# Token mixing's first matrix moved past tokens as weights, its output transposed through DRAM

## The chip, the cores and the metric

The kernel runs on one core of a Trainium2 chip. A core has five engines that run side by side, each in the order of its own instructions: TensorE (PE) for matmuls, VectorE (DVE), ScalarE (ACT) and GpSimd (POOL) for work on elements, and SyncE (SP), which here only issues DMA transfers. TensorE reads both operands from SBUF and writes to PSUM, eight banks of 2 KB per partition. The metric is the device time of one execution in microseconds, lower is better.

## What is computed

The input x is 2048 tokens by 448 channels. Branch A is attention with 16 query heads of 28 and one shared key and value head. Branch B is a mixer: token mixing, then an MLP. A gate from x mixes both. The part that matters here is token mixing:

```python
h = _gelu(_layernorm(x, axis=-1) @ w1)          # 448 x 448
c = D // 4
g0 = jnp.pad(h[:, :, 0*c:1*c], ((0, 0), (1, 0), (0, 0)))[:, :S, :]   # shift +1
g1 = jnp.pad(h[:, :, 1*c:2*c], ((0, 0), (0, 1), (0, 0)))[:, 1:, :]   # shift -1
...
hs = jnp.concatenate([g0, g1, g2, g3], axis=-1) @ w2
x1 = x + hs
```

Each quarter of the 112 channels of h is shifted by 1 or 2 tokens before w2.

## The kernel before, in words

Tokens are worked on in four blocks of 512 (`NB`), channels in four chunks of 128 (the last has 64 and carries the low part of its own in the other 64 partitions). Every product that needs precision is made from a high and a low part of each operand (`ah`/`al`, `w1h`/`w1l`, `hh`/`hl`), so that a block of `w1` takes 4 x 11 matmuls.

Stage 1 (lines 262 to 665) makes, on PE in the order of the program text:

- `stage_q(u)`, u = 0 to 15 (block times group of heads): queries, keys, values and the gate, with 11 matmuls each. `q_out` copies the result on ACT and sends it to DRAM (`qd`) from ACT's queue, the last one from SP's.
- `stage_w1(b)`, lines 442 to 468: h of block b, channels on partitions. For each of four groups of 112 channels, 11 matmuls with the weights of w1 as the stationary operand and 512 tokens moving; DVE multiplies by the inverse deviation of each token, which must stand along the free axis (`rsb`); ACT applies the gelu twice, once rounded (`hh`) and once not (`hf`); POOL subtracts (`hl`). The mean is taken out beforehand by centring w1 (`centre_w1`). `ln1_send` and `ln1_read` (lines 379 to 390) bring the deviations to that form: a PE transpose, an ACT copy, a write to DRAM and a broadcast read.
- `spare_h(b)` fills the 16 unused partitions of `hh` and `hl` with rows of the low part by four small DMAs, `spare_w2` does so for w2.
- `stage_w2(b)`, lines 470 to 482: for each of four tiles of 128 tokens, 11 matmuls of 448 columns with `hh`/`hl`, read at a shifted offset, as the stationary operand. The result is added to x1 by DVE. Its PSUM tiles come from `hs_tile`, which has two banks, so the third tile needs the add of the first.
- `stage_kv(b)`: eight DMAs that bring the keys of block b from `qd` to `kl` and two that bring values and gate to `vT`, on SP. `stage_v` transposes vT on PE.

`mm1` gives the PSUM tiles of `stage_q` and `stage_w1`, four in turn. The order of stage 1 is q0 to q11, w1(0), w1(1), w2(0), w1(2), w2(1), q12 to q15, w1(3), w2(2) with `stage_v` behind its first tile, w2(3). All engines keep the order of the program text (`manual_schedule`). Functions called `between` put work of other engines between the tiles of a stage.

The MLP's first input makes a similar trip already: `layernorm_norm` transposes blocks of 32 x 32 on DVE, `xt_write` writes them to DRAM in four DMAs (`xd`), `xt_read` reads them back with channels on partitions (`xr`), and `ln_split` copies them in a rearranged order.

Tiles with one tag share `bufs` buffers in turn; a new tile waits until the oldest is no longer used. Behind stage 1 come the MLP (lines 667 to 767) and the attention (from line 770), 785 us in which nothing of the text changes.

Of the kernel before, what the change touches and what calls it, by code (L numbers as in the profile page):

```python
# [9 lines left out]
F32 = mybir.dt.float32  # L10
F32R = mybir.dt.float32r
BF16 = mybir.dt.bfloat16
AF = mybir.ActivationFunctionType
ALU = mybir.AluOpType
# [3 lines left out]
P = 128  # L18
# [19 lines left out]
def f32(ap):  # L38
    return ap.bitcast(F32)
# [3 lines left out]
def gated_mix_kernel(  # L43
# [45 lines left out]
    def misc_tile(name):  # L89
        return psA.tile([P, 512], F32, tag="misc", bufs=1, name=name)  # L90
# [18 lines left out]
    def split_w_high(raw, wh, wl):  # L109
        nc.scalar.copy(wh[:, 0:3, :], raw[:, 0:3, :])  # L110
        nc.gpsimd.memset(f32(wh)[64:128, 3, :], 0.0)
        nc.scalar.copy(wh[0:64, 3, :], raw[0:64, 3, :])
        nc.scalar.copy(wl[64:128, 3, :], raw[64:128, 3, :])

    def split_w_low(raw, wh, wl):
        for c in range(3):
            nc.vector.tensor_tensor(wl[:, c, :], raw[:, c, :], f32(wh)[:, c, :], ALU.subtract)
        nc.vector.tensor_tensor(wl[0:64, 3, :], raw[0:64, 3, :], f32(wh)[0:64, 3, :], ALU.subtract)
# [14 lines left out]
    def proj(ps, wh, wl, ah, al):  # L133
        for c in range(3):
            nc.tensor.matmul(ps, wh[:, c, :], ah[:, c, :], start=(c == 0), stop=False)  # L135
            nc.tensor.matmul(ps, wh[:, c, :], al[:, c, :], start=False, stop=False)  # L136
            nc.tensor.matmul(ps, wl[:, c, :], ah[:, c, :], start=False, stop=False)  # L137
        nc.tensor.matmul(ps, wh[:, 3, :], ah[:, 3, :], start=False, stop=False)  # L138
        nc.tensor.matmul(ps, wl[:, 3, :], ah[:, 3, :], start=False, stop=True)  # L139
# [8 lines left out]
        nc.gpsimd.tensor_tensor(rs, rs, powt, ALU.pow)  # L148

    def stats_tiles(pool, b):  # L150
        return (pool.tile([P, 4, 2], F32, tag="mv", bufs=2, name=f"mv_{pool.name}_{b}"),
                pool.tile([P, 4], F32, tag="rs", bufs=2, name=f"rs_{pool.name}_{b}"))

    def layernorm_stats(pool, b):
        mv, rs = stats_tiles(pool, b)
# [106 lines left out]
    with tc.tile_pool(name="s1b", bufs=1) as s1b, \  # L262
# [5 lines left out]
        def mm1(name):  # L268
            k = turn[0] % 4
            turn[0] += 1  # L270
            return mm_tile(name) if k < 2 else ps1.tile([P, 512], F32, tag="tp", bufs=2, name=name)
# [6 lines left out]
        def load_x(b):  # L278
            if b == 1:
                xraw[b] = f32(s1b.tile([P, 4, 512], F32R, tag="w2x", bufs=1, name="xkv_1"))  # L280
            else:
                xraw[b] = s1.tile([P, 4, 512], F32, tag="raw", bufs=2, name=f"xkv_{b}")
            nc.sync.dma_start(xraw[b], xT[:, :, 512 * b:512 * b + 512])
# [12 lines left out]
            if c == 0:  # L296
                nc.sync.dma_start(wqraw[:, c, 256:512], wq[:, c, 256:512])
        nc.scalar.activation(first, powt, AF.Gelu_apprx_tanh)
        w1h = s1.tile([P, 4, 512], F32R, name="w1h")
        w1l = s1.tile([P, 4, 512], F32R, name="w1l")  # L300
        w2h = s1b.tile([P, 4, D], F32R, name="w2h")
        w2l = s1b.tile([P, 4, D], F32R, name="w2l")
        hh, hl, acts = {}, {}, {}
# [61 lines left out]
            nc.vector.tensor_copy(vext[:, :, 1:1 + DH].rearrange("p (b t) d -> p t b d", t=4), vp[:, :, :, 0:DH])  # L365
            nc.vector.tensor_copy(gz.rearrange("p (b t) -> p t b", t=4), vp[:, :, :, DH])

        rb_of = {}

        rs1_of = {}  # L370

        def ln1_tile(b, t):
# [2 lines left out]
            stats_tile(s1, b, t, rs1_of[b][0])  # L375
            if t == 3:
                stats_end(*rs1_of[b])

        def ln1_send(b):
            ps = misc_tile(f"rsT_{b}")[0:4, 0:P]  # L380
            nc.tensor.transpose(ps, rs1_of.pop(b)[1], ident)
            rT = s1.tile([4, P], F32, tag="rT", bufs=2, name=f"rT_{b}")
            nc.scalar.copy(rT, ps)
            rb_of[b] = dram.tile([4, P], F32, tag="rsd", bufs=2, name=f"rsd_{b}")
            nc.sync.dma_start(rb_of[b], rT)

        def ln1_read(b):
            rd = rb_of[b]
            rb_of[b] = s1.tile([P, 512], F32, tag="rsb", bufs=2, name=f"rsb_{b}")
            nc.sync.dma_start(rb_of[b][0:C], rd.rearrange("(o t) p -> o (t p)", o=1).broadcast_to([C, 512]))  # L390

        ones = s1.tile([P, P], F32, name="ones")
        nc.gpsimd.memset(ones, 1.0)
# [16 lines left out]
        def high_w2(m):  # L410
            nc.scalar.copy(w2h[0:C, m, :], w2raw[0:C, m, :])
            if m:
                nc.gpsimd.tensor_copy(w2x[0:C, m, :], f32(w2h)[0:C, m, :])

        def spare_w2():
            high = f32(w2h)
            nc.sync.dma_start(high[C:P, 0:2, :], high[0:32, 0, :])
            nc.sync.dma_start(high[C:P, 2:4, :], high[32:64, 0, :])
            nc.sync.dma_start(f32(w2x)[C:P, 1:3, :], high[64:96, 0, :])
            nc.sync.dma_start(f32(w2x)[C:P, 3, :], high[96:112, 0, :])  # L420
# [11 lines left out]
        def spare_h(b):  # L432
            low = f32(hl[b])
            nc.sync.dma_start(shifted(hh[b], 0, 2), low[0:32, 0, 1:513])
            nc.sync.dma_start(shifted(hh[b], 2, 2), low[32:64, 0, 1:513])
            nc.sync.dma_start(shifted(hl[b], 1, 2), low[64:96, 0, 1:513])
            nc.sync.dma_start(shifted(hl[b], 3, 1), low[96:112, 0, 1:513])

        def low_w2(m):
            nc.vector.tensor_tensor(w2l[0:C, m, :], w2raw[0:C, m, :], f32(w2h)[0:C, m, :], ALU.subtract)  # L440

        def stage_w1(b, between=None):
            hh[b] = s1b.tile([P, 4, 516], F32R, tag="hh", bufs=2, name=f"hh_{b}")
            hl[b] = s1b.tile([P, 4, 516], F32R, tag="hl", bufs=2, name=f"hl_{b}")
            for tt in (hh, hl):
                if b == 0:
                    nc.gpsimd.memset(f32(tt[b])[0:C, :, 0:2], 0.0)
                else:
                    nc.gpsimd.tensor_copy(tt[b][0:C, :, 0:2], f32(tt[b - 1])[0:C, :, 512:514])
            for m in range(4):  # L450
                ps = mm1(f"h_{b}_{m}")
                w = slice(m * P, m * P + C)
                proj(ps[0:C, :], w1h[:, :, w], w1l[:, :, w], *xact[b])
                if between:
                    between(m)
                hf = s1.tile([P, 512], F32, tag="hf", bufs=3, name=f"hf_{b}_{m}")
                nc.vector.tensor_mul(hf[0:C, :], ps[0:C, :], rb_of[b][0:C, :])
                nc.scalar.activation(hh[b][0:C, m, 2:514], hf[0:C, :], AF.Gelu_apprx_tanh)
                nc.scalar.activation(hf[0:C, :], hf[0:C, :], AF.Gelu_apprx_tanh)
                nc.gpsimd.tensor_tensor(hl[b][0:C, m, 2:514], hf[0:C, :], f32(hh[b])[0:C, m, 2:514],  # L460
                                        ALU.subtract)
            if b in (0, 2):
                spare_h(b)
            for tt in (hh, hl):
                if b:
                    nc.gpsimd.tensor_copy(tt[b - 1][0:C, :, 514:516], f32(tt[b])[0:C, :, 2:4])
                if b == NB - 1:
                    nc.gpsimd.memset(f32(tt[b])[0:C, :, 514:516], 0.0)

        def stage_w2(b, between=None):  # L470
            for t in range(4):
# [42 lines left out]
        centre_w1()  # L514
        stage_q(7)
        stage_q(8)
        w1_views = [f32(w1raw).rearrange("p c (m j) -> p c m j", j=C)]
        w1_views += [w.rearrange("p c (m j) -> p c m j", j=P)[:, :, :, 0:C] for w in (w1h, w1l)]
        split_w_high(*w1_views)
        split_w_low(*w1_views)  # L520
        for t in range(4):
            ln1_tile(1, t)
        stage_q(9)
        ln1_send(0)
        ln1_read(0)
        load_x(3)
        stage_q(10)
        load_x1(3)
        stage_q(11)
        high_w2(0)  # L530
        high_w2(1)

        def first_between(m):
            low_w2(m)
            if m < 2:
                high_w2(m + 2)
            if m == 2:
                ln1_send(1)
                ln1_read(1)
                spare_w2()  # L540

        stage_w1(0, first_between)

        def second(m):
            if m < 2:
                high_x(3, 2 * m, 2 * m + 2)
            if m in (1, 2):
                split_x(3, 2 * m - 2, 2 * m, False)
            else:
                ln1_tile(2, 2 * m // 3)  # L550
                ln1_tile(2, 2 * m // 3 + 1)

        stage_w1(1, second)
        stage_kv(0)
        stage_kv(1)
        spare_h(1)

        def third(t):
            if t == 2:
                ln1_send(2)  # L560
                ln1_read(2)
            if t < 3:
                ln1_tile(3, t)

        stage_w2(0, third)
        stage_kv(2)
        ln1_tile(3, 3)
        mv0, rs0 = stats_tiles(s1, "m")
        stage_w1(2, lambda t: stats_tile(s1, 0, t, mv0))
        stats_end(mv0, rs0)  # L570
        ln1_send(3)
        ln1_read(3)
        xt4 = s1.tile([P, 2048], F32, tag="raw", bufs=2, name="xt4")[:, 0:4 * D].rearrange(
            "p (f t j) -> p f t j", f=NE, t=4)

# [3 lines left out]

        stage_w2(1, norm_first)  # L580
        xt_write(0, xt4)
        for u in range(12, 16):
            stage_q(u)
        stage_w1(3)
        stage_kv(3)
        s1_stack.close()

# [54 lines left out]

        xraw2[0] = big("xr_0").rearrange("p (c n) -> p c n", c=4)
        xt_read(0, xraw2[0])
        spare_h(NB - 1)
        load_w34(0, s2a)

        def third(t):
# [496 lines left out]
```

## Time and profile before

| | |
|---|---|
| median of 3 runs | 911.44 us (911.14 to 912.0) |
| span of the profiled execution | 909.7 us |
| PE, share of the span busy | 99% |
| ACT | 70% |
| DVE | 57% |
| POOL | 9% |

The span runs from the first to the last instruction of the profiled execution; the page gives no other time of that execution, and the runs' times include what lies around the span.

A row of a timeline has the start in us, the duration in us, the engine, the line of the kernel, the operation, output<-input, shape and count, and in brackets the idle time before it and what ended it. A row of a group has the count, then the busy time and the mean duration in ns, then the idle time of the engine before its instructions and the releasers. A row of waits has the total in us, the number of times and the longest. `SPq` and `ACTq` are the queues from which SP and ACT issue DMAs. Matmuls overlap, so that their durations are longer than the distance of their starts.

### The profile page before, as it was taken

The numbers are of one execution on the slowest core, as the hardware profiler recorded it, in microseconds if no ns is written. First come the engines' busy times: TensorE is split into PE (matmuls) and PEld (weight loads), VectorE is DVE, ScalarE is ACT, GpSimd is POOL, SyncE is SP. The second block draws the span as 40 slices with busy tenths as digits, with TensorE's granted clock in tenths as the row PEclk, the third lists the DMA queues.
The fourth block names the chain that finished last, engine by engine and source line by source line (L and its number), as shares of the span: only waits on it lengthen the run. The fifth ranks groups of instructions, "written<-read, shape, count | busy, mean of one in ns | idle before, by whom it ended". The sixth has DMA issues, their size and how long they took to land.

```text
span 909.7 us, 24149 instructions
## 1 busy us (share of the span) xinstructions
PE 903.1 (99%) x10360; PEld 626.8 (69%) x10360; DVE 515.8 (57%) x960; ACT 632.6 (70%) x1003; POOL 79.1 (9%) x116
## 2 busy tenths in 40 slices
PE   9999999999999999999999999999999999999998
PEld 6788888888888888875555555555555555555554
DVE  3665273631441531136766777676767667767665
ACT  5542444332132231269999999999999999999995
POOL 3243320200000520020000000000000000000000
PEclk9999999999999999999999999999999999999999
DMA  8832653120110120010000001000011000010001
GB/s 294 289 103 61 147 167 129 37 70 1 39 49 2 22 65 1 1 52 24 14 25 14 24 15 56 23 25 17 25 33 36 24 14 25 15 55 14 15 14 44
DMA packets 40726, 47.31 MB, mean 52 GB/s; under 512 B 10152, under 2 KB 28904, under 8 KB 40616
## 3 DMA queue, kind: packets, MB, share of 16 engines
q1 hardware_dynamic: 37448, 40.43, 15.2%
q10 hardware_dynamic: 3168, 5.31, 1.6%
q8 instruction: 82, 1.34, 0.6%
q14 instruction: 28, 0.23, 0.1%
HBM read 32.56 MB, written 11.67 MB: 49 GB/s over the span
## 4 chain that ended last, share of the span: by engine, by line
PE 97%; ACT 2%; DMA 1%; DVE 0%; issue 0%; SPq 0%
PE bank L893 26%; PE bank L204 20%; PE bank L844 6%; PE acc L701 5%; PE acc L699 5%; PE acc L700 5%; PE g L135 4%; PE g L137 4%; PE g L136 4%; PE pair L204 2%; ACT p L257 2%; PE hs L475 1%; PE hs L476 1%; PE g L138 1%; PE g L139 1%; PE h L136 1%
## 5 line engine op out<-in xcount | busy, mean ns | idle before, releaser
L257 ACT ACTIVATE p<-bank 128x512 f32<-128x512 f32 x514 | 265.9, 605 | 4.4 <-POOL pick L866 1.5
L893 PE MATMUL bank<-p,vext 128*32 128x256 f32 x4064 | 247.7, 382 | 1.0 <-ACT p L257 1.0
L893 PEld LDWEIGHTS bank<-p,vext 128*32 128x32 f32 x4064 | 117.9, 110 | 115.9 <-ACT p L257 53.0
L954 DVE COPY p<-pair 128x1024 f32<-128x1024 f32 x125 | 153.0, 1224 | 57.9 <-PE pair L204 40.9
L689 ACT ACTIVATE gh<-g 128x512 fp32r<-128x512 f32 x55 | 32.9, 598 | 181.7 <-PE g L139 181.7
L818 DVE TENSOR_TENSOR o<-o,bank 128x256 f32<-128x256 f32 x222 | 93.5, 421 | 80.4 <-PE bank L893 72.3
L257 ACT ACTIVATE p<-p 128x1024 f32<-128x1024 f32 x126 | 138.0, 1096 | 0.0
L257 ACT ACTIVATE p<-pair 128x1024 f32<-128x1024 f32 x129 | 136.8, 1060 | 0.0
L691 DVE TENSOR_TENSOR gl<-gf,gh 128x512 fp32r<-128x512 f32 x55 | 38.6, 702 | 164.9 <-ACT gf L690 164.9
L204 PE MATMUL bank<-qh,kh 32*128 32x512 f32 x514 | 114.8, 443 | 0.0
L204 PE MATMUL pair<-qh,kh 32*128 32x512 f32 x510 | 114.0, 443 | 0.0
L204 PE MATMUL bank<-qh,kl 32*128 32x512 f32 x514 | 101.8, 389 | 0.0
L204 PE MATMUL bank<-ql,kh 32*128 32x512 f32 x514 | 101.6, 390 | 0.0
L204 PE MATMUL pair<-qh,kl 32*128 32x512 f32 x510 | 101.3, 389 | 0.0
L204 PE MATMUL pair<-ql,kh 32*128 32x512 f32 x510 | 100.9, 389 | 0.0
L204 PEld LDWEIGHTS bank<-qh,kh 32*128 32x128 f32 x514 | 48.0, 182 | 61.3 <-issue 38.7
L701 PE MATMUL acc<-w4h,gl 128*128 128x448 f32 x220 | 80.7, 367 | 0.0
L699 PE MATMUL acc<-w4h,gh 128*128 128x448 f32 x220 | 80.2, 364 | 0.0
L700 PE MATMUL acc<-w4l,gh 128*128 128x448 f32 x220 | 79.8, 363 | 0.0
L844 PE MATMUL bank<-wof,on 128*32 128x224 f32 (+1 forms) x984 | 69.6, 357 | 0.0
L135 PE MATMUL g<-ah,w3h 128*128 128x512 f32 x168 | 65.4, 389 | 0.0
L136 PE MATMUL g<-al,w3h 128*128 128x512 f32 x168 | 65.4, 389 | 0.0
(206 smaller groups left out, 1394.1 us busy)
## 6 DMA issues: line engine op xcount, KB each, us to landing
qd<-qf ACTq DMA_DIRECT2D x15, 256.0 KB
rb<-rd SPq DMA_DIRECT2D x15, 256.0 KB
x<-in_x_dram SPq DMA_DIRECT2D x4, 896.0 KB
xd<-xt SPq DMA_DIRECT2D x16, 224.0 KB
w34raw<-in_w_dram SPq DMA_DIRECT2D x7, 512.0 KB
qr<-qd SPq DMA_DIRECT2D x64, 56.0 KB
w34raw<-in_w_dram SPq DMA_DIRECT2D x7, 448.0 KB
out_dram<-ot SPq DMA_DIRECT2D x14, 224.0 KB
```

What stands on the lines that cost most here:

```text
L135: nc.tensor.matmul(ps, wh[:, c, :], ah[:, c, :], start=(c == 0), stop=False)
L136: nc.tensor.matmul(ps, wh[:, c, :], al[:, c, :], start=False, stop=False)
L204: nc.tensor.matmul(ps[j], k[h, keys], q[h, :], start=(r == 0), stop=(r == 2), tile_position=(32 * j, 0))
L257: nc.scalar.activation(p[:, heads], p[:, heads] if source is None else source, AF.Exp, scale=SCALE)
L691: nc.vector.tensor_sub(gl, gf, f32(gh))
L699: nc.tensor.matmul(ps, gh[:, tok], w4h[i][:, k, :], start=(f == 0), stop=False)
L700: nc.tensor.matmul(ps, gh[:, tok], w4l[i][:, k, :], start=False, stop=False)
L701: nc.tensor.matmul(ps, gl[:, tok], w4h[i][:, k, :], start=False, stop=(f == stop))
L818: nc.vector.tensor_add(o, o, pv)
L844: nc.tensor.matmul(ps[32 * i:32 * i + 32, :], a[:, c:c + 32], w, start=start, stop=stop, tile_position=(0, 32 * i))
L893: nc.tensor.matmul(pv[32 * j:32 * j + 32, :], vext[:, kt, :], p_of[k][:, j, qs], start=(k == ks[0]), stop=(k == ks[-1]), tile_position=(0, ...
L954: nc.vector.tensor_copy(pa[:, both], pairs[0])
```

## The change

The operands of w1's product change sides: a tile of 128 tokens of x is the stationary operand, and the 448 columns of w1 move, so that h comes out with tokens on partitions. The inverse deviation is then one number per partition and goes into the gelu's `scale`. `ln1_send`, `ln1_read` and their tiles are gone. DVE transposes h in blocks of 32 x 32 into `ht`; four DMAs write it to DRAM (`hd`), one reads it back with channels on partitions (`h_read`, into `hraw`, one buffer); `h_part` copies it into `hh` on ACT and subtracts into `hl` on DVE (even groups) or POOL (odd ones). `spare_h` is now issued behind the first group.

The order becomes q0 to q11, w1(0), w1(1), w1(2), q12, w2(0), w1(3), w2(1), q13 to q15, w2(2), w2(3); `stage_kv` of blocks 0 to 2 moves ahead of w1(0). x of block 3 is loaded into a buffer of `hraw`'s, `w1h` and `w1l` get 448 columns instead of 512, and `mv` and `rs` a third buffer.

```diff
         def load_x(b):
...
+            elif b == 3:
+                xraw[b] = s1.tile([P, 4, 512], F32, tag="hraw", bufs=1, name="xkv_3")
...
-        def stage_w1(b, between=None):
+        hd_of, hraw_of = {}, {}
+
+        def stage_w1(b, between=None, after=None):
+            ht = s1.tile([P, 2048], F32, tag="raw", bufs=2, name=f"ht_{b}")[:, 0:4 * D].rearrange(
+                "p (f t j) -> p f t j", f=NE, t=4)
+            ah, al = xact[b]
+            for t in range(4):
+                tok = slice(t * P, (t + 1) * P)
+                ps = mm1(f"h_{b}_{t}")[:, 0:D]
+                for c in range(3):
+                    nc.tensor.matmul(ps, ah[:, c, tok], w1h[:, c, :], start=(c == 0), stop=False)
+                    nc.tensor.matmul(ps, al[:, c, tok], w1h[:, c, :], start=False, stop=False)
+                    nc.tensor.matmul(ps, ah[:, c, tok], w1l[:, c, :], start=False, stop=False)
+                nc.tensor.matmul(ps, ah[:, 3, tok], w1h[:, 3, :], start=False, stop=False)
+                nc.tensor.matmul(ps, ah[:, 3, tok], w1l[:, 3, :], start=False, stop=True)
+                if between:
+                    between(t)
+                hf = s1.tile([P, 512], F32, tag="hf", bufs=3, name=f"hf_{b}_{t}")[:, 0:D]
+                nc.scalar.activation(hf, ps, AF.Gelu_apprx_tanh, scale=rs1_of[b][1][:, t:t + 1])
+                nc.vector.transpose(ht[:, :, t, :], hf.rearrange("p (f j) -> p f j", j=32))
+                if after:
+                    after(t)
+            hd_of[b] = dram.tile([NE, 32, 4, 128], F32, tag="hd", bufs=2, name=f"hd_{b}")
+            for p in range(4):
+                nc.sync.dma_start(hd_of[b][:, :, p].rearrange("f i u -> i f u"),
+                                  ht[32 * p:32 * p + 32].rearrange("i f t j -> i f (t j)"))
+
+        def h_read(b):
+            hraw_of[b] = s1.tile([P, 4, 512], F32, tag="hraw", bufs=1, name=f"hraw_{b}")
+            nc.sync.dma_start(hraw_of[b][0:C], hd_of.pop(b).rearrange("f i p u -> (f i) (p u)").rearrange(
+                "(m r) u -> r m u", m=4))
...
-            for m in range(4):
-                ps = mm1(f"h_{b}_{m}")
...
+        def h_part(b, m):
+            raw = hraw_of[b][0:C, m, :].rearrange("n (p t j) -> n p t j", p=4, t=4)
+            hi, lo = [tt[b][0:C, m, 2:514].rearrange("n (t p j) -> n p t j", p=4, t=4) for tt in (hh, hl)]
+            nc.scalar.copy(hi, raw)
+            (nc.gpsimd if m % 2 else nc.vector).tensor_tensor(lo, raw, f32(hi), ALU.subtract)
+
+        def h_parts(b, m0, m1):
+            if m0 == 0:
+                h_begin(b)
+            for m in range(m0, m1):
+                h_part(b, m)
+                if m == 0:
+                    spare_h(b)
...
         high_w2(0)
         high_w2(1)
+        for b in range(3):
+            stage_kv(b)
...
+        stage_w1(0, in_first)
+        h_read(0)
...
+        stage_w1(1, in_second)
+        stage_w1(2, None, lambda t: t in (1, 2) and h_parts(0, 2 * t - 2, 2 * t))
+        h_read(1)
+        stage_q(12)
+
+        def in_w2_first(t):
+            if t < 2:
+                h_parts(1, 2 * t, 2 * t + 2)
             if t < 3:
                 ln1_tile(3, t)
 
-        stage_w2(0, third)
-        stage_kv(2)
+        stage_w2(0, in_w2_first)
         ln1_tile(3, 3)
+        h_read(2)
         mv0, rs0 = stats_tiles(s1, "m")
-        stage_w1(2, lambda t: stats_tile(s1, 0, t, mv0))
+        stage_w1(3, lambda t: stats_tile(s1, 0, t, mv0), lambda t: t < 2 and h_parts(2, 2 * t, 2 * t + 2))
         stats_end(mv0, rs0)
-        ln1_send(3)
-        ln1_read(3)
+        h_read(3)
...
         stage_w2(1, norm_first)
         xt_write(0, xt4)
-        for u in range(12, 16):
-            stage_q(u)
-        stage_w1(3)
+        stage_q(13)
+        h_parts(3, 0, 2)
+        stage_q(14)
+        h_parts(3, 2, 4)
+        stage_q(15)
         stage_kv(3)
         s1_stack.close()
```

More of the change, by code (lines that the diff above doesn't have):

```diff
@@ L150, in stats_tiles @@
     def stats_tiles(pool, b):
-        return (pool.tile([P, 4, 2], F32, tag="mv", bufs=2, name=f"mv_{pool.name}_{b}"),
-                pool.tile([P, 4], F32, tag="rs", bufs=2, name=f"rs_{pool.name}_{b}"))
+        return (pool.tile([P, 4, 2], F32, tag="mv", bufs=3 if pool.name == "s1" else 2, name=f"mv_{pool.name}_{b}"),
+                pool.tile([P, 4], F32, tag="rs", bufs=3 if pool.name == "s1" else 2, name=f"rs_{pool.name}_{b}"))
     def layernorm_stats(pool, b):
@@ L298, in gated_mix_kernel @@
         nc.scalar.activation(first, powt, AF.Gelu_apprx_tanh)
-        w1h = s1.tile([P, 4, 512], F32R, name="w1h")
-        w1l = s1.tile([P, 4, 512], F32R, name="w1l")
+        s1.tile([P, 16], F32, name="gap_w1")
+        w1h = s1.tile([P, 4, D], F32R, name="w1h")
+        w1l = s1.tile([P, 4, D], F32R, name="w1l")
+        s1.tile([P, 48], F32, name="gap_x")
         w2h = s1b.tile([P, 4, D], F32R, name="w2h")
@@ L366, in stage_v @@
             nc.vector.tensor_copy(gz.rearrange("p (b t) -> p t b", t=4), vp[:, :, :, DH])
-        rb_of = {}
         rs1_of = {}
@@ L377, in ln1_tile @@
                 stats_end(*rs1_of[b])
[L379 to L390, printed above, removed]
         ones = s1.tile([P, P], F32, name="ones")
@@ L440, in low_w2, with h_begin @@
             nc.vector.tensor_tensor(w2l[0:C, m, :], w2raw[0:C, m, :], f32(w2h)[0:C, m, :], ALU.subtract)
-        def stage_w1(b, between=None):
+        hd_of, hraw_of = {}, {}
[27 more added lines that the diff above has]
+                "(m r) u -> r m u", m=4))
+        def h_begin(b):
             hh[b] = s1b.tile([P, 4, 516], F32R, tag="hh", bufs=2, name=f"hh_{b}")
@@ L449, in stage_w1 @@
                     nc.gpsimd.tensor_copy(tt[b][0:C, :, 0:2], f32(tt[b - 1])[0:C, :, 512:514])
-            for m in range(4):
-                ps = mm1(f"h_{b}_{m}")
[L452 to L468, printed above, removed]
+        def h_part(b, m):
[10 more added lines that the diff above has]
+                    spare_h(b)
+            if m1 == 4:
+                for tt in (hh, hl):
+                    if b:
+                        nc.gpsimd.tensor_copy(tt[b - 1][0:C, :, 514:516], f32(tt[b])[0:C, :, 2:4])
+                    if b == NB - 1:
+                        nc.gpsimd.memset(f32(tt[b])[0:C, :, 514:516], 0.0)
         def stage_w2(b, between=None):
@@ L516, in gated_mix_kernel @@
         stage_q(8)
[L517 to L520, printed above, removed]
+        split_w_high(w1raw, w1h, w1l)
+        split_w_low(w1raw, w1h, w1l)
         for t in range(4):
@@ L523, in gated_mix_kernel @@
         stage_q(9)
-        ln1_send(0)
-        ln1_read(0)
         load_x(3)
@@ L531, in gated_mix_kernel, with in_first, in_second @@
         high_w2(1)
[L533 to L539, printed above, removed]
-                spare_w2()
[L542 to L561, printed above, removed]
+        for b in range(3):
+            stage_kv(b)
+        def in_first(t):
+            low_w2(t)
+            if t < 2:
+                high_w2(t + 2)
+            if t == 2:
+                spare_w2()
+            if t == 3:
+                ln1_tile(2, 0)
+                ln1_tile(2, 1)
+        stage_w1(0, in_first)
+        h_read(0)
+        def in_second(t):
+            if t < 2:
+                high_x(3, 2 * t, 2 * t + 2)
+            if t in (1, 2):
+                split_x(3, 2 * t - 2, 2 * t, False)
+            if t in (0, 3):
+                ln1_tile(2, 2 + t // 3)
+        stage_w1(1, in_second)
[3 more added lines that the diff above has]
+        def in_w2_first(t):
+            if t < 2:
+                h_parts(1, 2 * t, 2 * t + 2)
             if t < 3:
                 ln1_tile(3, t)
-        stage_w2(0, third)
-        stage_kv(2)
+        stage_w2(0, in_w2_first)
         ln1_tile(3, 3)
+        h_read(2)
         mv0, rs0 = stats_tiles(s1, "m")
-        stage_w1(2, lambda t: stats_tile(s1, 0, t, mv0))
+        stage_w1(3, lambda t: stats_tile(s1, 0, t, mv0), lambda t: t < 2 and h_parts(2, 2 * t, 2 * t + 2))
         stats_end(mv0, rs0)
-        ln1_send(3)
-        ln1_read(3)
+        h_read(3)
         xt4 = s1.tile([P, 2048], F32, tag="raw", bufs=2, name="xt4")[:, 0:4 * D].rearrange(
@@ L644, in gated_mix_kernel @@
         xt_read(0, xraw2[0])
-        spare_h(NB - 1)
         load_w34(0, s2a)
```

## The prediction

> **What bounds the kernel now.** I read the page first, then stage 1 (0 to 125 us), the only stretch that the change touches, engine by engine in time.
>
> ```profile
> span 909.7 us, 24149 instructions
> PE   9999999999999999999999999999999999999998
> PE 97%; ACT 2%; DMA 1%; DVE 0%; issue 0%; SPq 0%
> ```
>
> PE is busy in every slice and makes 97% of the chain that ended last. The span is the profiled execution's own; the runs' median, 911.44, is 1.7 above it, and I add changes of the span to the median. As nothing ends later than PE, an edit is worth what it changes in PE's own time plus every wait that it puts in front of PE. PE takes its work in program order, so a wait of one matmul is a wait of all behind it.
>
> PE's timeline (start, duration, line) gives the pace as the distance of starts, since the durations overlap:
>
> ```profile
> 44.22 0.39 PE L139 MATMUL h<-ahk,w1l 128*112 128x512 f32 x1
> ...
> 44.47 0.48 PE L135 MATMUL h<-ahk,w1h 128*112 128x512 f32 x1
> 44.78 0.40 PE L136 MATMUL h<-alk,w1h 128*112 128x512 f32 x1
> ...
> 57.15 0.37 PE L475 MATMUL hs<-w2h,hh 128*128 128x448 f32 x1
> ...
> 63.90 0.27 PE L381 MATMUL rsT<-ident,rs_s 128*4 128x128 f32 x1
> ...
> 95.77 0.39 PE L135 MATMUL h<-ahk,w1h 128*112 128x512 f32 x1
> ...
> 105.86 0.36 PE L475 MATMUL hs<-w2h,hh 128*128 128x448 f32 x1
> ...
> 108.10 0.60 PE L363 MATMUL vp<-ident,vT 128*128 128x128 f32 x4
> ```
>
> From 95.77 to 105.86 run the 44 matmuls of one w1 block, 512 columns each: 10.09 / 44 = 0.2293 us. From 57.15 to 63.90 run 33 of w2, 448 columns with 128 weight columns, the shape that w1 gets: 6.75 / 33 = 0.2045 us. Around 44.4 two matmuls and a transpose (rsT) take 44.22 to 44.78 = 0.56, of which two matmuls are 0.46: a transpose costs 0.10.
>
> **PE's own work.** 4 blocks x 44 matmuls go from 0.2293 to 0.2045: 176 x 0.0248 = 4.4 us less; 4 transposes x 0.10 = 0.4 less. Together **-4.8 us**. Blocks now take 9.0 us.
>
> **ACT, DVE and POOL.** What they do beside it, in groups of the first 250 us (count, busy us, mean ns):
>
> ```profile
> L457 DVE TENSOR_TENSOR hf<-h,rsb 112x512 f32<-112x512 f32 x16 | 11.0, 689 | 26.8 <-PE h L139 18.5 <-DMA rsb<-rsd 7.1 <-PE rsT L381 1.1
> L458 ACT ACTIVATE hh<-hf 112x512 fp32r<-112x512 f32 x16 | 10.1, 632 | 23.8 <-DVE hf L457 23.8
> L164 DVE STREAM_TRANSPOSE xt<-xn 128x448 f32<-128x448 f32 x12 | 7.8, 646 | 0.4
> L143 DVE BATCH_NORM_STATS2 st_s<-x 128x6 f32<-128x448 f32 x20 | 12.1, 607 | 0.0
> L480 DVE TENSOR_TENSOR x<-x,hs 128x448 f32<-128x448 f32 x16 | 9.8, 612 | 8.8 <-PE hs L478 8.8
> L144 DVE BATCH_NORM_AGGREGATE mv_s<-st_s 128x2 f32<-128x6 f32 x16 | 2.9, 182 | 0.5
> L636 ACT CAST ah<-xr 128x512 fp32r<-128x512 f32 x8 | 4.5, 619 | 4.6 <-DMA xr<-xd 4.5
> ```
>
> DVE loses 16 multiplies of 0.69 and gets 16 transposes of 0.65 (the form of L164) and 8 subtractions that POOL did. ACT loses 32 gelus of 0.63 and gets 16 gelus (448/512 of 0.63, 0.55 by estimate) and 16 copies in four-level order (L636, 0.62). The multiply's waits on rsb (7.1 us) go; PE never stood for them. In amount all this is covered by idle time (L457 and L458 alone sat idle 26.8 and 23.8 us). What counts is the order, since h now goes through DRAM, and ACT and DVE wait for its return ahead of work that PE needs.
>
> **The price of the round trip.** The rows of xd/xr have the same layout as hd/hraw (start, duration on SP; ACT's release):
>
> ```profile
> 24.34 0.38 SPq L286 DMA_DIRECT2D x<-in_x_dram  x1
> 54.47 3.45 SPq L349 DMA_DIRECT2D kl<-qd  x8
> 57.96 0.80 SPq L352 DMA_DIRECT2D vT<-qd  x2
> 58.80 3.29 SPq L349 DMA_DIRECT2D kl<-qd  x8
> 96.58 0.35 SPq L321 DMA_DIRECT2D qd<-qf  x1
> 96.98 3.31 SPq L349 DMA_DIRECT2D kl<-qd  x8
> 100.33 0.80 SPq L352 DMA_DIRECT2D vT<-qd  x2
> 105.35 0.38 SPq L176 DMA_DIRECT2D xr<-xd  x1
> 107.03 0.60 SPq L434 DMA_DIRECT2D hh<-hl  x1
> 109.58 0.61 SPq L612 DMA_DIRECT2D w34raw<-in_w_dram  x1
> 176.69 3.02 SPq L171 DMA_DIRECT2D xd<-xt  x4
> 183.16 0.38 SPq L176 DMA_DIRECT2D xr<-xd  x1
> ```
>
> ```profile
> 110.64 2.36 ACT L636 CAST ah<-xr 128x512 fp32r<-128x512 f32 x4 [2.42 <-DMA xr<-xd]
> ```
>
> Writing: the four issues take 3.0 us, and the read that needs them goes out 183.16 - 176.69 = 6.5 us after the first. Reading: issued at 105.35, ACT released at 110.64: 5.3 us. Round trip 11.8.
>
> A view in windows (DMA share and GB/s last) shows why the write is slow:
>
> ```profile
> 33.00:34.00 1.00, 1.00 (x6) 0.81 (x5) 0.00 (x0) 0.98 (x1) 0.00 (x0) 1.00 1.06 406
> 89.00:89.50 0.50, 0.50 (x4) 0.42 (x3) 0.00 (x0) 0.08 (x1) 0.00 (x0) 1.00 0.98 174
> ```
>
> While xd is written (89 us) the DMA engines are full at 174 GB/s; loads fill them at 406 (33 us). The Trainium skill, "DMA: Bandwidth & Descriptors", Specifications, puts the smallest transfer for line rate at 512 B, which these pieces of 128 floats just meet; by it 0.92 MB would take 2.3 us at 406 GB/s and each write end some 3 us sooner, wait A below would fall to about 0.4 and the sum to +0.7. The trace disagrees, 174 against 406 GB/s, and the sum goes by the trace.
>
> **Wait A, in w2 of block 0.** PE goes on at 36.8 and ends w1 blocks 0, 1, 2 at 45.8, 54.8, 63.8, q12 at 66.3, and the first three tiles of w2(0) at 68.6, 70.8 and 73.1 (11 x 0.2045 = 2.25 each). Tile 3 needs the PSUM bank of tile 1 (two hs banks), so DVE's add of tile 1. Ahead of that add stands the subtraction of h_parts(1,0), which needs ACT's copy, which needs h_read(1). In the best case the gelu and transpose of w1(2)'s last tile are done at 65.3; the writes of hd_2, four issues, stand ahead of h_read(1) on SP: issue 68.3, landing 73.6. Then copy 0.62, subtraction 0.8, statistics 0.61 + 0.18, add 0.61: 76.5 instead of 73.1, **3.4 us at least**.
>
> SP may be late already. The waits of SP's queue:
>
> ```profile
> SPq L286 <- DMA x<-in_x_dram: 8.8, 1, 8.8
> SPq L385 <- DMA w2raw<-in_w_dram: 8.2, 1, 8.2
> SPq L390 <- DMA rsd<-rT: 5.2, 4, 1.9
> ```
>
> The issue of x for block 2 (24.34) stood 8.8 us until an earlier load had landed, though it needs none of its data: an issue waits for a landing some eight transfers back. The engines are full to 34.8; xkv_3 and x1(3), 1.92 MB, now follow at once, 4.8 us at 406 GB/s, with three qd writes until about 41. The 30 small issues of stage_kv(0..2) that were moved here cost 3 x (58.80 - 54.47) = 13.0 us, and only the first few can pass before x1(3) lands. They end near 50 to 51, then come four of spare_w2 (109.58 - 107.03 = 2.6), so hd_0 goes out between 47.2 (when it is ready) and 54. I take 52: hraw_0 at 63.8. ACT stands for it ahead of two gelus of w1(2), then does four copies and two gelus (2.5 + 1.1), DVE the last transpose: hd_2 at 68.1, h_read(1) landing near 76.6, the add done at 79.4: **A = 6.3** (3.4 to 8.3). A part of it may stand before tile 0 already, whose first matmuls read rows of hh_0 that spare_h(0) brings.
>
> **Wait B, in w2 of block 2.** Before, q15 ends at 95.77, its copy leaves on SP at 96.58, and eight kl and two vT issues follow, the last starting near 100.73. The transposes of vT come only at 108.10, because w1(3) lay between. Now w1(3) is earlier, and between q15 and them stands one tile of w2, 2.25 us. When the last vT lands no row shows; the shortest landing is that of a 2 KB row (L390, 5.2 / 4 = 1.3), the longest likely one that of a 224 KB read, under 2.9; I take 1.9: 102.6, which is 6.9 after q15's end. Wait 6.9 - 2.25 = 4.6 (3.9 to 5.6). h_read(3) lands 13.8 after w1(3) ends (2.0 + 11.8); copy, subtraction and four spare_h(3) issues end at 17.8, and q15's output is ready at 9.0 + 7.5 + 0.8 = 17.3: 0.5 more. **B = 5.1** (3.9 to 6.5). The transposes' own wait is all that PE sees: what follows (xr, w3/w4 loads) moves with SP and keeps its 16 us ahead of the first g matmul.
>
> **Sum:** -4.8 + 6.3 + 5.1 = +6.6 us on the span: 911.4 + 6.6 = **918.0**. With the bounds: -4.8 + 3.4 + 3.9 = +2.5 (913.9) to -4.8 + 8.3 + 6.5 = +10.0 (921.4).
>
> **Rivals.**
> 1. *The round trip gets home in time* (not slower). If h_read(1) lands by 70.2, 1.9 us after its issue, the add isn't late and A is gone; B alone gives -4.8 + 5.1 = +0.3: 911.7. For it: a 2 KB write lands in 1.3 us. Against it: 5.3 us at 105.35 and writes at 174 GB/s ahead of it. To be faster by 0.2% (1.8 us) B would have to be under 3.0 as well, less than the issues alone take.
> 2. *PE runs slowly after each wait.* At the start of the kernel 20 matmuls of 256 columns take 3.7 us:
>
> ```profile
> 0.77 3.71 PE L97 MATMUL warm_ps<-const-bfloat16-1.0 128*128 128x256 bf16 x20 [0.77 <-PEq L1133]
> ```
>
> That is 256 / 0.185 = 1380 columns per us against 448 / 0.2045 = 2190 later. If PE falls back so after each wait of 4 us or more, the 3.7 us that follow do the work of 2.3, 1.4 lost, twice: 918.0 + 2.8 = 920.8. Against it: the granted clock stands at 1.00 in every window, and no wait like it is in the trace. The Trainium skill, "TensorE: Matmul & The Clock Gate", Part 1, says so: half clock after an idle window of about 3.4 us, until one busy window has passed.
> 3. *ACT stands early.* If a q output's issue on ACT has to wait for xkv_3 (landing about 38), the copies that make w1h come 3 us late and PE waits at 36.8: 921. For it: that issues wait for older loads; against: most slots hit none.
> 4. *The matmuls don't get shorter* (the pace is set by the 128-column weight load, not by the 448 columns): no 4.4, 922.4. Against it: 0.2045 in w2, with the same weights' shape.
>
> **How the numbers follow.** Forecast 0.52; rival 1 0.18, rival 2 0.18, rival 3 0.08, rival 4 0.04. About 0.2% is what a measurement of this kernel can tell from no change. Rival 1 gives same 0.10, faster 0.06, slower 0.02; all others are slower: faster 0.06, same 0.10, slower 0.84. The range for 8 in 10 runs from 911.2, which takes in most of rival 1, to 922.0, past rivals 2 and 3.
>
> **What would show it.** PE's h group at 0.2045 a matmul with 448 columns; one idle time of PE before w2(0)'s last tile, released by the add L480, with DVE in turn released by ACT's copy and that by DMA hraw; one before vp, released by DMA vT. The forecast is wrong if hd's four writes and the read take under 8 us, if SP issues hd_0 before 48 us (A is then 3.4), or if PE shows no idle time before vp.

## The result, and the profile after

The changed kernel takes **935.0 us** (median; 933.95 to 936.32), the kernel before 911.72 (911.14 to 912.0) beside it: a ratio of **1.0254** (1.0242 to 1.0267). The direction was forecast; the size was not: +6.6 us were forecast and +23 came, past the upper end of the range.

From the page of the changed kernel, its span, the 40 slices of PE and of PE's granted clock, and the chain that ended last:

```profile
span 932.3 us, 24155 instructions
PE   9986969999999999999999999999999999999997
PEclk9996989999999999999999999999999999999999
PE 85%; DMA 2%; ACT 2%; SPq 1%; DVE 0%; issue 0%; POOL 0%; ACTq 0%
```

PE is no longer busy throughout: slices 3, 4 and 6 (47 to 93 and 117 to 140 us, at 23.3 us each) have holes, and in 4 and 6 the granted clock, 9 tenths or more in every slice before, is lower. PE's share of the chain falls from 97% to 85%. The view of waits puts the holes into three places (total, times, longest):

```profile
PE vp L367 <- DMA vT<-qd: 7.3, 1, 7.3
PE hs L497 <- POOL hl L476: 6.5, 1, 6.5
PE hs L497 <- DVE x L502: 6.3, 1, 6.3
PE hs L497 <- POOL hh L488: 0.2, 1, 0.2
```

PE's timeline places them (start, duration, line; in brackets the idle time before and what ended it):

```profile
36.82 0.37 PE L441 MATMUL h<-w1h,ahk 128*128 128x448 f32 x1
...
63.23 0.39 PE L135 MATMUL q<-ahk,wqh 128*128 128x512 f32 x1
...
72.41 0.71 PE L497 MATMUL hs<-w2h,hh 128*128 128x448 f32 x1 [6.50 <-POOL hl L476]
...
87.71 0.74 PE L497 MATMUL hs<-w2h,hh 128*128 128x448 f32 x1 [6.28 <-DVE x L502]
...
128.41 1.09 PE L367 MATMUL vp<-ident,vT 128*128 128x128 f32 x4 [7.32 <-DMA vT<-qd]
...
146.14 0.39 PE L135 MATMUL g<-ah,w3h 128*128 128x512 f32 x1
```

At 72.41 w2(0) begins, at 87.71 its last tile, at 128.41 the transposes of vT. The first matmul of the MLP starts at 146.14 instead of 124.66: 21.5 of the 22.6 us of span are lost by then. From 36.82 to 63.23 run 132 matmuls of w1: 26.41 / 132 = 0.2001 us each, against 0.2293 before.

Windows of the changed kernel (length, busy time and count of PE, PEld, DVE, ACT, POOL, then PE's granted clock, DMA share, GB/s):

```profile
72.50:76.60 4.10, 4.10 (x11) 3.67 (x12) 0.00 (x0) 0.00 (x0) 0.17 (x2) 0.50 0.72 174
87.80:94.00 6.20, 6.03 (x15) 4.93 (x16) 4.24 (x9) 0.00 (x0) 1.34 (x3) 0.50 0.67 179
129.20:131.50 2.30, 2.30 (x8) 2.08 (x7) 0.72 (x2) 0.00 (x0) 2.22 (x3) 0.50 0.99 339
```

Behind each of the three waits the clock is 0.50, and matmuls start 0.37 us apart (11 in 4.1 us), where at full clock they start 0.20 apart.

**The account.** The stretch from the first w1 matmul to the first g matmul, from PE's timeline: "waits" is the idle time in brackets; "slow" is what single matmuls took from start to start beyond the full-speed pace of their kind (0.2001 for the new w1, 0.2293 for the old one, 0.206 for w2, 0.227 for q), where that is over 0.06 us; "own" is the rest. The kernels e5 to e9 are those of the experiments below.

| us | stretch | own | waits | slow |
|---|---|---|---|---|
| before | 87.8 | 87.2 | 0 | 0.6 |
| after | 109.3 | 82.3 | 20.3 | 6.8 |
| e5, no trip | 97.1 | 82.3 | 10.5 | 4.2 |
| e7 | 97.7 | 82.1 | 11.5 | 4.1 |
| e8 | 88.5 | 81.8 | 3.9 | 2.8 |
| e9 | 83.4 | 81.7 | 0.8 | 0.9 |

The change does save what it was charged for, 4.9 us, and pays 20.3 in waits and 6.2 in clock. About 1 us of a single wait is scatter between executions: the first one, 6.5 here, is 5.5 in e1 and 7.2 in e4, whose order up to there is the same.

**Where the waits come from.** SP's timeline of the changed kernel (start, duration, line, count), a row of its waits between 30 and 44 us, and ACT's two releases:

```profile
32.06 11.26 SPq L353 DMA_DIRECT2D kl<-qd  x8
...
56.33 3.24 SPq L455 DMA_DIRECT2D hd<-ht  x4
62.94 0.30 SPq L460 DMA_DIRECT2D hraw<-hd  x1
...
72.52 4.14 SPq L455 DMA_DIRECT2D hd<-ht  x4
76.76 1.20 SPq L460 DMA_DIRECT2D hraw<-hd  x1
...
121.75 0.53 SPq L325 DMA_DIRECT2D qd<-qf  x1
122.72 3.19 SPq L353 DMA_DIRECT2D kl<-qd  x8
```

```profile
SPq L353 <- DMA qd<-qf: 5.7, 4, 2.1
```

```profile
68.52 1.14 ACT L475 CAST hh<-hraw 112x512 fp32r<-112x512 f32 x2 [8.86 <-DMA hraw<-hd]
...
84.99 2.18 ACT L475 CAST hh<-hraw 112x512 fp32r<-112x512 f32 x4 [12.75 <-DMA hraw<-hd]
```

h_0 leaves at 56.33: the first eight of the 30 copies of `stage_kv` alone hold SP for 11.26 us, half of it in waits for the landing of outputs of `stage_q`, which ACT issues. Its trip ends at 68.52 (12.2 us), and the parts are ready only for 72.41. The trip of h_1, behind the stores of h_2 on SP, is read from 76.76 on and home at 84.99: 8.2 us, not 5.3.

### The profile page after: what moved, and what is told of

Read it like the earlier page. It is cut to its first block, busy times and chain, and to the rows that moved or that the text cites. A ratio compares the mean times of both kernels' runs of the same rounds, so it can differ in the third digit from the quotient of the medians.

```text
span 932.3 us, 24155 instructions
## 1 busy us (share of the span) xinstructions
PE 905.4 (97%) x10356; PEld 633.4 (68%) x10356; DVE 518.5 (56%) x968; ACT 630.3 (68%) x999; POOL 69.3 (7%) x108
## 4 chain that ended last, share of the span: by engine, by line
PE 85%; DMA 2%; ACT 2%; SPq 1%; DVE 0%; issue 0%; POOL 0%; ACTq 0%
PE bank L913 25%; PE bank L204 19%; PE bank L864 5%; PE acc L721 5%; PE acc L719 5%; PE acc L720 5%; PE g L136 4%; PE g L137 4%; PE g L135 4%; PE pair L204 2%; ACT p L257 2%; PE g L138 1%; PE g L139 1%; PE hs L497 1%; PE hs L498 1%; PE hs L500 1%
```

## The experiments

**e1: the transposes of vT one stage later.** `stage_v` moves from the first tile of w2(2) to the first of w2(3).

```diff
         def third(t):
-            if t == 0:
-                stage_v()
-            elif t > 1:
+            if t > 1:
                 ln_split(0, 2 * t - 4, 2 * t - 2)
...
         def weights(t):
+            if t == 0:
+                stage_v()
```

> stage_v (the PE transposes of vT) stands at the first tile of w2(3) instead of w2(2); nothing is left out. Theory: PE's 7.5 us of idle time before vp and the half-clock matmuls behind it (8 matmuls, 1.9 us with the transposes) are the wait for vT and go. Next late is xr: DVE's add of w2(2)'s last tile stands behind ln_split's subtraction, which waits for xr (ACT at 131.8 in the changed kernel), and w2(3)'s second tile needs that bank: about 4 us come back. 935.0 - 9.4 + 4 = about 929.6. Rival (the stop belongs to w2(2), whatever stands there): as much idle time at w2(2)'s second tile, 935.

Measured: 931.79 us (ratio 1.0222, 1.0205 to 1.0239). PE's timeline:

```profile
127.90 0.60 PE L367 MATMUL vp<-ident,vT 128*128 128x128 f32 x4
132.48 0.74 PE L497 MATMUL hs<-w2h,hh 128*128 128x448 f32 x1 [3.98 <-DVE x L502]
```

The transposes no longer wait. But the next tile does, 4.0 us, for an addition that stands on DVE behind the splits of xr, which SP had also sent late. Wait B was a wait for SP's queue, and taking away its first customer shows the second: 3.2 us were gained, not the 7.3 of the wait. The forecast of 929.6 missed by 2.2 us: it had let the half clock go with the wait, and behind the new wait it came back (7.8 us of "slow" in e1, counted as in the account, against 6.8 in the changed kernel).

**e2: PE kept busy in the holes.** 28, 36 and 32 matmuls on data nobody reads, ahead of the first and last tile of w2(0) and of the transposes.

```diff
+        def busy(n):
+            ps = misc_tile(f"busy_{n}")[:, 0:D]
+            for _ in range(n):
+                nc.tensor.matmul(ps, w2h[:, 1, 0:P], w2h[:, 2, :], start=True, stop=True)
...
+                if b == 0 and t in (0, 3):
+                    busy(28 if t == 0 else 36)
```

> Adds 28, 36 and 32 matmuls of 448 columns into an unused PSUM bank before w2(0)'s first tile, before its last tile, and before the transposes of vT; the output is unchanged. They fill most of PE's three waits (5.7, 7.4 and 6.5 us) and should end before them. Theory (the granted clock falls to one half in a wait, and the matmuls behind it are slow for that): the granted clock stays at 1.00, matmuls behind the waits start every 0.205 us, not 0.372. The slow stretch before the second wait is hidden in that wait, so only those behind the second and third come back: 935.0 - 3.2 - 1.9 = about 930. Rival (the slow matmuls wait for their operands): the stretches stay at 0.37 us, 935 or more.

Measured: 930.03 us (ratio 1.0207, 1.0190 to 1.0224). The windows behind the three places now show clock 1.00; one of them:

```profile
88.00:92.00 4.00, 3.35 (x17) 2.98 (x17) 3.70 (x8) 0.00 (x0) 0.95 (x3) 1.00 0.67 169
```

The tiles start when they did (72.94 and 87.49 instead of 72.41 and 87.71), g at 141.70 instead of 146.14. So 4.4 us by g, 5.0 by the medians, are the half clock alone; the 2.1 us behind the first wait were hidden, since they only shortened the second.

**e3: the key copies behind the trips.** `stage_kv(0)` to `(2)` go from ahead of w1(0) to behind `h_read(2)`.

```diff
-        for b in range(3):
-            stage_kv(b)
...
         h_read(2)
+        for b in range(3):
+            stage_kv(b)
```

> The 30 transfers of stage_kv(0) to stage_kv(2) move from ahead of w1(0) to behind h_read(2); nothing is left out. Theory (SP's queue makes hd_0 late, 56.3 instead of about 50): hd_0 goes out when its transposes are done (50.0), hraw_0 lands near 62.7 instead of 68.5, PE's wait before w2(0) falls from 6.7 to about 1 us, the last tile of w2(0) starts near 82 instead of 87.7: 935.0 - 5.9 = about 929. Rival (the round trip alone is too long, whenever it starts): the start of w2(0) stays near 72, 935.

Measured: 943.55 us (ratio 1.0341, 1.0323 to 1.0359): the total missed, the first half did not. SP's and PE's timelines:

```profile
47.18 3.07 SPq L455 DMA_DIRECT2D hd<-ht  x4
...
98.48 11.59 SPq L356 DMA_DIRECT2D vT<-qd  x2
```

```profile
65.44 0.37 PE L497 MATMUL hs<-w2h,hh 128*128 128x448 f32 x1
...
81.07 0.74 PE L497 MATMUL hs<-w2h,hh 128*128 128x448 f32 x1 [8.70 <-DVE x L502]
...
135.96 1.09 PE L367 MATMUL vp<-ident,vT 128*128 128x128 f32 x4 [20.47 <-DMA vT<-qd]
```

h_0 leaves at 47.18, when it is ready; w2(0) starts without a wait, its last tile 6.6 us earlier. The first wait was SP's lateness. The last tile still waits 8.7 us, for the trip of h_1. Then SP stands 10.9 us in the row of 98.48, ahead of the last copy of block 2, which turns the 7.3 us before the transposes into 20.5. The row of SP's waits, and the ACT row that ended it:

```profile
SPq L356 <- DMA qd<-qf: 10.9, 1, 10.9
```

```profile
107.42 0.33 ACTq L325 DMA_DIRECT2D qd<-qf  x1
```

The transfer that it stood for is the output of q13, in block 3, whose data these copies do not need. In the trace the transfers of SP and ACT take eight semaphores in turn, in planned order, and one that gets a semaphore waits until the transfer eight places back has landed: the copy that stood has that of q13's output, and its row ends at 110.07, 2.65 us after that output was issued. So SP's queue can stand for a transfer of ACT's, here one that ACT could only issue once PE had done q13.

**e4: the additions of w2(0) ahead of the subtractions.** `h_parts(1)` one tile later, so that the addition of tile 1 has no subtraction of h_1 ahead of it, the order on DVE that the prediction gave as the reason for wait A.

```diff
-            if t < 2:
-                h_parts(1, 2 * t, 2 * t + 2)
+            if t in (1, 2):
+                h_parts(1, 2 * t - 2, 2 * t)
```

> h_parts(1) stands one tile later in w2(0), so that DVE's add of tile 1 comes before the subtraction that waits for hraw_1; nothing is left out. As predicted (PSUM bank of tile 1): the bank is free in time and the 6.4 us before the last tile go, with the slow matmuls behind them, 935.0 - 9 = about 926. Rival (the last tile of block 0 also reads two tokens of block 1, which POOL copies over only behind h_parts(1)): the wait stays and ends with POOL's copy, about 89: 935 to 936.

Measured: 935.27 us (ratio 1.0257, 1.0240 to 1.0274): nothing gained. The last tile of w2(0):

```profile
90.30 0.74 PE L497 MATMUL hs<-w2h,hh 128*128 128x448 f32 x1 [6.50 <-POOL hh L488]
```

It now waits for L488, POOL's copy of h_1's first tokens into `hh_0`. A group shifted back by 1 or 2 tokens needs them, so the last tile of every block but the fourth needs the trip of the next block, in whatever order DVE works. In the changed kernel the two came close together: the bank held the tile until 87.71, and its third matmul then waited 0.2 us more for L488 (the last row in the view of waits above).

**e5: no trip at all.**

```diff
-            hd_of[b] = dram.tile([NE, 32, 4, 128], F32, tag="hd", bufs=2, name=f"hd_{b}")
-            for p in range(4):
-                nc.sync.dma_start(hd_of[b][:, :, p].rearrange("f i u -> i f u"),
-                                  ht[32 * p:32 * p + 32].rearrange("i f t j -> i f (t j)"))
...
-            nc.sync.dma_start(hraw_of[b][0:C], hd_of.pop(b).rearrange("f i p u -> (f i) (p u)").rearrange(
-                "(m r) u -> r m u", m=4))
+            nc.sync.dma_start(hraw_of[b][0:C], xT[0:C, :, 512 * b:512 * b + 512])
```

> Leaves the round trip of h out: the 16 stores of h_d are gone, and the read that filled hraw takes the same bytes from the input xT, so the token mixing's second matrix works on other numbers. Everything else, the transposed first matrix with its gelu and VectorE's transposes included, stays as in the changed kernel. Theory (the trip through DRAM, with the SyncE time that its stores take, is the whole loss, and TensorE's own work is about 4.9 us shorter): w1(0) to w1(2) keep 0.200 us a matmul, no wait over 1 us before w2(0), its last tile or vp, no stretch at a granted clock of 0.5 behind them, 907 to 909 us, faster than before by 3 to 5. Rival (something else of the change costs as well: the gelu on tokens, VectorE's transposes, the new buffers, the 1.1 us in the attention): 911 us or more, with the excess in groups other than the three waits.

Measured: 921.26 us (ratio 1.0097, 1.0076 to 1.0117). Both theories missed: the excess lies in the three places after all, but the trip is not the whole of it.

```profile
PE vp L367 <- DMA vT<-qd: 6.3, 1, 6.3
PE hs L492 <- DVE x L497: 2.7, 1, 2.7
PE hs L492 <- POOL hl L471: 0.9, 1, 0.9
PE hs L492 <- POOL hh L483: 0.6, 1, 0.6
```

In w2(0) 4.2 us are left of 13.0: a read and the copies and subtractions behind it are still needed, one block's buffer at a time. Wait B stays almost whole, so the trip does not cause it. SP's timeline there:

```profile
106.54 1.81 SPq L424 DMA_DIRECT2D hh<-hl  x1
...
109.81 0.53 SPq L325 DMA_DIRECT2D qd<-qf  x1
110.51 3.19 SPq L353 DMA_DIRECT2D kl<-qd  x8
```

q15's copy was done at 108.13, its output goes out at 109.81 behind the spare copies of h_3, and ten key and value copies follow. B comes from w1(3) having moved ahead of q13 to q15, which leaves one tile of w2 between q15 and the transposes. This is read from the order; e7 to e9, where two blocks of w2 and a tile lie there, have no wait before the transposes.

**e7: the order that covers the trip.** w1(0) to w1(3) in a row, q12 to q15, then w2(0) to w2(3); the read of h_1 ahead of the stores of h_3, key copies later.

```diff
+        stage_w1(2, lambda t: ln1_tile(3, t))
+        stage_w1(3, None, lambda t: t in (0, 1) and h_parts(0, 2 * t, 2 * t + 2), lambda: h_read(1))
         stage_q(12)
+        stage_q(13)
+        h_parts(1, 0, 2)
+        stage_q(14)
+        h_parts(1, 2, 4)
         h_read(2)
+        stage_kv(1)
+        stage_q(15)
...
+        stage_w2(0, lambda t: stats_tile(s1, 0, t, mv0))
+        stage_kv(2)
+        stage_kv(3)
```

> The changed kernel's arithmetic in another order: w1(0) to w1(3), then the query groups 12 to 15, then w2(0) to w2(3); the read of h_1 stands ahead of the stores of h_3, the copies of k and v behind the reads (kv(0) behind that of h_0, kv(1) behind that of h_2, kv(2) and kv(3) behind w2(0)). Between the last matmul of w1(0) and the first of w2(0) TensorE then has about 36 us of work instead of 20. Theory (the round trip is a latency of 16 to 20 us that costs only where TensorE has no other work): no wait over 1 us before w2(0) or its last tile, 905 to 911 us. Rival (SyncE's one queue is full: 16 stores, 16 spare copies, 40 k and v copies at about 0.3 us each and more where one waits for the transfer eight back): the wait comes back before w2(1), w2(2) or xr, 915 to 925 us.

Measured: 923.46 us (ratio 1.0136, 1.0115 to 1.0157), as the rival said. w2(0) has one wait of 0.9 us left, and three of 0.9 to 2.1 us lie in w2(1) to w2(3). The one of 5.9 is new, for the spare rows of h_2, which SP issues at 105.99 behind 20 copies of `stage_kv` (waits of PE, then SP's timeline):

```profile
PE hs L499 <- DMA hh<-hl: 5.9, 1, 5.9
```

```profile
97.55 3.30 SPq L353 DMA_DIRECT2D kl<-qd  x8
100.90 0.81 SPq L356 DMA_DIRECT2D vT<-qd  x2
101.75 3.29 SPq L353 DMA_DIRECT2D kl<-qd  x8
105.08 0.80 SPq L356 DMA_DIRECT2D vT<-qd  x2
105.99 0.58 SPq L423 DMA_DIRECT2D hh<-hl  x1
```

**e8: the same with SP's queue relieved.** Key copies of blocks 0 to 2 back ahead of w1(0), now harmless since h_0 is needed only at 82 us; `stage_kv(3)` right behind q15; the outputs of q12 to q15 on SP's queue, so that no transfer of SP's stands for one of ACT's.

```diff
-            (nc.sync if u == NU - 1 else nc.scalar).dma_start(qd[g, :, 512 * b:512 * b + 512], qf)
+            (nc.sync if u >= 12 else nc.scalar).dma_start(qd[g, :, 512 * b:512 * b + 512], qf)
```

> As e7, with less on SyncE's queue where e7 lost its 5.9 us (the four spare copies of h_2 behind 30 copies of k and v): kv(0) to kv(2) are back ahead of w1(0), kv(3) behind the output of q15, and the outputs of q12 to q15 go out on SyncE's queue instead of ScalarE's, so that no transfer of SyncE's has a transfer of ScalarE's eight places ahead of it. Theory (the two waits of the change were latency without other TensorE work, and e7's was SyncE's queue): no PE wait over 1.5 us before w2(0), w2(1), w2(2) or vp, g starts at 119 to 122 us (before 124.7), 906 to 911 us. Rival (SyncE's queue is still what is late: h_0 leaves at 56 us again, and the read of h_1 and the spare copies follow it by the same 9 us): a wait of 3 to 6 us before the last tile of w2(0) or in w2(1), 914 to 920 us.

Measured: 912.86 us (ratio 1.0015, 1.0006 to 1.0024), 0.15 per cent above before. w2(0), w2(1) and the transposes do not wait. But the forecast of 906 to 911 missed: two waits of together 3.5 us lie in w2(2) and w2(3), and 1.4 us of half clock (8 matmuls at 0.37) behind the first:

```profile
PE hs L499 <- DVE x L504: 3.5, 2, 2.0
```

**e9: and the additions free.** On DVE the subtractions of h_3 stand behind the additions of the first two tiles of w2(2), and the splits of xr behind additions of w2(3). The read of xr and the first loads of w3 and w4 move behind the first tile of w2(2), `stage_v` to its third.

```diff
         def third(t):
+            if t < 2:
+                h_parts(3, 2 * t, 2 * t + 2)
             if t == 0:
+                xt_read(0, xraw2[0])
+                load_w34(0, s2a)
+            if t == 2:
                 stage_v()
-            elif t > 1:
-                ln_split(0, 2 * t - 4, 2 * t - 2)
...
-            if t % 2 == 0:
-                split_w3(t // 2)
-            else:
-                split_w4(t // 2)
-                load_w34(t // 2 + 1, s2a)
+            if t < 2:
+                ln_split(0, 2 * t, 2 * t + 2)
+            else:
+                split_w3(t - 2)
+                split_w4(t - 2)
+                load_w34(t - 1, s2a)
```

> As e8, with VectorE's order in w2(2) and w2(3) changed: the subtractions of h_3 stand behind the additions of tiles 0 and 1 of w2(2) (in e8 all of them stood ahead of w2(2)), and the splits of the fourth stage's activations behind the additions of tiles 0 and 1 of w2(3) instead of those of tiles 2 and 3 of w2(2), with those of w3 and w4 after them. Theory (e8's two waits of 2.0 and 1.5 us and the 1.4 us at half clock are additions held behind VectorE work that waits for DRAM): both waits go, w2(2) and w2(3) take 18.5 to 19.5 us instead of 21.9, g starts at 121 to 123 us, 908 to 911 us, faster than before by 0.1 to 0.4 per cent. Rival (the last round trip, that of block 0's normalised x, is late anyway, so the wait only moves to the first g): g at 124 to 125.5 us, 911 to 913 us.

Measured: **909.76 us, ratio 0.9975 (0.9965 to 0.9985)**, a quarter of a per cent faster than before. PE's waits in all of stage 1 and the start of the MLP:

```profile
PE g L135 <- ACT gf L709: 1.4, 1, 1.4
PE hs L499 <- DVE x L504: 0.7, 1, 0.7
PE hs L499 <- POOL hh L490: 0.2, 1, 0.2
```

g starts at 120.76, 3.9 us before the old kernel's 124.66, and gives back 1.4 at once, waiting for ACT. So the change of operands is worth its few microseconds once the trip lies behind other matmuls. The new order alone can't be the gain: the kernel before has no waits in this stretch (0 in the account), and "own" falls from 87.2 to 81.7.

## Why the prediction was wrong

- **PE's own work, -4.8: right.** 82.3 against 87.2 is -4.9 (the pace is 0.2001 a matmul, a little under the 0.2045 taken from w2). What is left to the 5.4 that this pace and three transposes give is mainly the transposes of vT, at half clock in the changed kernel; e9 has 81.7, which is -5.5. Rival 4 is out.
- **Wait A, +6.3 (3.4 to 8.3): this step failed, in size and in reason.** It came to 13.0 us. "SP may be late already" was right, but h_0 left at 56.33, past the bound of 54: the 30 copies ended at 53.49, not at 50 to 51. With a trip of 12.2 us (11.8 forecast) that made a wait of 6.5 already ahead of tile 0, which the prediction knew of only as a "part" of one wait; e3 shows that it is SP's lateness, since it is gone when h_0 leaves at 47.18. The wait before the last tile was expected, at the right place, but for the bank on DVE's order; e4 shows that the tile needs h_1 itself through L488. That it measured the 6.3 of the forecast is luck: the forecast had no long wait ahead of it, and the tile started at 87.71 instead of 73.1 + 6.3 = 79.4. And the read of h_1 took 8.2 us where 5.3 were taken from the row of xr.
- **Wait B, +5.1 (3.9 to 6.5): right in place and reason, under-sized.** It measured 7.3, and the upper bound of 6.5 is itself more than its terms give (5.6 + 0.5 = 6.1). q15's output left SP at 121.75, 3.1 us after q15's end (118.66 in PE's timeline), not 1.3; e5 shows the same wait without any trip. That what follows on SP "keeps its 16 us" was also wrong: e1 met a wait of 4.0 for xr.
- **Half clock: a rival that should have been a term.** It was given 0.18 and two stretches of 1.4 us, "against it: the granted clock stands at 1.00 in every window". But, as it says itself, no such wait was in that trace, so that row could say nothing about what follows a wait. All three waits were followed by clock 0.50, 6.2 us in the account and 4.4 to 5.0 in e2. The Trainium skill, "TensorE: Matmul & The Clock Gate", Part 1, which the prediction named beside this rival, puts half clock behind an idle window of about 3.4 us. The trace agrees on the half clock (0.50), but not on the idle time: 1.7 us in such a window were enough (last section).
- **Rival 1 (the trip home in time) and rival 3 (ACT early) are out:** the trip took 12.2 us, and w1(0) started at 36.82 against 36.89. From the first store of h_0 to the issue of its read went 6.6 us (56.33 to 62.94), as the row of xd had said (6.5). The store some 3 us shorter, which the prediction estimated from the Trainium skill, "DMA: Bandwidth & Descriptors", Specifications (512 B as the smallest transfer for line rate), did not show.
- The sum: -4.9 + 20.3 + 6.2 = +21.6 on the stretch. The last 1.1 us of the span lie in the MLP and the attention. The single executions of the changed kernel span 932.1 to 934.5, so a remainder of this size is within their scatter; its cause stays open.

## What to carry to other kernels

A matmul made shorter by a new layout is worth its saving only if the path that brings the new layout home has that much other TensorE work behind it: count the whole trip, from the queue that issues it to the last consumer, the neighbour block's halo included, and place it first. Price each wait of about 2 us or more with the half clock that follows it, even if the trace of before never shows a clock below 1.00. And when many small copies are moved ahead in one queue, whatever is issued behind them is late by their sum.

## What the runs showed of the hardware

- The half clock comes in pieces of 3.41 us. By the clock records of the traces, every stretch of it between 30 and 150 us lasts 3.41, 6.83 or 10.24 us (23.89 in e3), one, two, three or seven pieces. Cut into such pieces, counted from where the clock changes, all ten traces read alike in these 120 us: a full-clock piece in which PE was idle for 1.7 us or more (1.7 in e3, 1.8 in e8, 2.1 in e5) was followed by half clock, one with 1.6 us or less (1.6 twice in e7) was not. So a wait much shorter than those above can bring it, late, and where it falls decides: e8's wait of 2.0 us until 108.12 lies almost whole in one piece, e7's of 2.1 us until 118.48 is split over two. Where between 1.6 and 1.7 us the limit lies no run here shows. Pieces of e8, then of e7 (length, PE's busy time; the clock stands third from the end):

```profile
106.32:109.73 3.41, 1.60 (x8) 1.49 (x9) 2.88 (x5) 0.50 (x1) 3.33 (x8) 1.00 0.93 183
109.73:113.15 3.42, 3.42 (x11) 3.04 (x10) 0.62 (x1) 0.00 (x0) 3.34 (x4) 0.50 0.54 164
```

```profile
114.54:117.95 3.41, 1.83 (x9) 1.33 (x8) 1.95 (x3) 2.18 (x4) 1.73 (x2) 1.00 0.72 210
117.95:121.37 3.42, 2.89 (x14) 2.69 (x15) 1.96 (x5) 0.00 (x0) 3.34 (x8) 1.00 0.40 115
```

- With the operands exchanged, the same number of multiplications took 0.2001 us a matmul instead of 0.2293, a factor of 0.873; the moving columns went from 512 to 448, a factor of 0.875.
